# Beacon attention and soft-MoE slots: loading q and k as four rows per partition, a shorter write stride in the evacuation, earlier weight loads, output tiles in the weight slots

## The chip, the cores and the metric

The kernel runs on one core of one Trainium2 chip. The metric is the device time of one execution in microseconds, as the median of several runs. A profile is one of these executions, and its span is about 2 us shorter than the time. Each run is marked fast or slow (slow: more than 1.5% above the fastest run of the same kernel). Medians are taken over all runs.

## The reference

Causal attention with 16 beacon tokens in front, for 64 heads of 576 tokens and 64 features; then a soft mixture of experts over all 4608 tokens.

```python
# q, k, v: (8, 8, 576, 64)   beacon_k, beacon_v: (8, 8, 16, 64)   float32
scores = scale * (q @ concat([beacon_k, k]).T)        # causal over k, beacons always seen
a = softmax(scores)
x = (a @ concat([beacon_v, v])) -> (4608, 512)
logits = x @ phi                                      # phi: (512, 32), 8 experts x 4 slots
slot_input = softmax(logits, axis=0).T @ x            # 32 x 512
slot_out[e] = relu(slot_input[e] @ w1[e]) @ w2[e]     # w1: (8,512,1024), w2: (8,1024,512)
out = softmax(logits, axis=1) @ slot_out
```

TensorE needs q and k with features on the partitions, so each pair of heads is transposed. The 32 weight pieces are 1 MiB of float32 each in HBM, cast to float16 on the way. The output is 9.4 MB.

## The kernel before

A pair of heads is loaded with the 64 partitions of a head holding nine successive rows each (2304 contiguous bytes). TensorE transposes the nine 64x64 pieces per head into PSUM (the memory for TensorE's results; the kernel keeps its other tiles in SBUF), as `tp[feature, j, s]`, where token `9*s + j` is wanted. The copy to SBUF, called the evacuation below, puts the tokens in order.

```python
def load_pair(n):
    b, g = divmod(n, H // 2)
    for (d, src, nm) in ((qf, q, "qf"), (kf, k, "kf")):
        t = qkp.tile([P, J, D], FP, name=nm, tag=nm)          # J = 9, 5 buffers
        nc.sync.dma_start(out=t[:, :, :],
            in_=src[b, 2*g:2*g+2].rearrange("h s d -> (h s) d").rearrange("(p j) d -> p j d", j=J))
        d[n] = t
# ...
def transp(n):
    for (f, dst) in ((qf, qT[n % 3]), (kf, kT[n % 3])):
        t = f.pop(n)
        tp = ps_tr.tile([P, J, 64], BF, name="tr", tag="tr")
        for j in range(J):
            for po in (0, 64):
                nc.tensor.transpose(tp[po:po+64, j, :], t[po:po+64, j, :].bitcast(BF)[:, 1::2], ...)
        nc.vector.tensor_copy(                                 # writes every 9th element: 18 bytes
            out=dst[:, Nb:Nb + S].rearrange("p (s j) -> p j s", j=J), in_=tp[:, :, :])
    nc.gpsimd.tensor_copy(out=kT[n % 3][:, 0:Nb], in_=bkT[:, n, :])
# ...
for n in range(NP + 1):                    # 32 pairs; the attention of pair n-1 runs beside the scores of n
    b, g = divmod(n, H // 2)
    score(n, 0); score(n, 1)
    transp(n + 1)
    attend(n - 1, 0)                       # ends in a reciprocal and a product (xb) on VectorE
    score(n, 2)
    attend(n - 1, 1)
    # ... routing pieces of the finished batch ...
    score(n, 3)
    load_pair(n + 5)
    load_v(b + 1, g)
    for c in ((), (0, 1), (2,), (3, 4))[g]:
        cast_v(b + 1, c)                   # even c on GpSimd, odd c on VectorE
    if n % 2 == 1 and n >= 5:              # 14 weight loads, issued from GpSimd
        load_w(wl); wl += 1
# ... experts: 24 weight pieces fit in six pairs of slots, the last 8 wait for freed slots ...
for cg in range(NG):
    osb = exq.tile([P, G, Dm], FP, name="osb", tag="ex", bufs=2)
    # ... two tiles by ScalarE, two by VectorE, then a 1 MB store ...
```

The softmax here doesn't subtract the row's maximum and nothing guards it: scores larger than these inputs give would overflow.

## Time and profile before

| | before |
|---|---|
| time, median of 3 runs | 426.59 us (424.94 to 427.09) |
| span of the profiled run | 424.7 us |
| loop of 32 pairs / closing routing / experts / output | 316 / 15.8 / 41.2 / 33.7 us |
| VectorE busy | 249.9 us, of it 179 us in the 64 evacuations |

The stages, by windows cut at the events that separate them. Columns: window, length, then busy time of each engine with its number of instructions, the granted clock of TensorE, the mean share of the 16 DMA engines, and GB/s.

```profile
core 0: us, PE busy (x) PEld busy (x) DVE busy (x) ACT busy (x) POOL busy (x), PEclk, DMA share, GB/s
18.00:334.00 316.00, 173.99 (x2944) 134.95 (x2946) 222.85 (x245) 110.70 (x151) 69.38 (x131) 0.63 0.43 100
334.00:349.80 15.80, 12.12 (x192) 9.71 (x187) 6.03 (x23) 4.51 (x10) 9.38 (x13) 0.61 0.82 135
349.80:391.00 41.20, 28.39 (x323) 13.95 (x321) 0.57 (x2) 1.58 (x8) 5.82 (x8) 0.71 1.09 192
391.00:424.70 33.70, 16.74 (x37) 4.74 (x36) 13.64 (x19) 11.88 (x18) 0.00 (x0) 0.50 0.68 280
```

In the loop VectorE is the busiest engine (222.85 of 316 us), and DMA has room (share 0.43). In the expert stage the DMA share is 1.09, and waits for weights stand in the chain. Next, the chain that ended last, in one pair of the loop (start, duration, what):

```profile
...
190.21 0.64 PE tr L188 x12
...
190.88 2.70 DVE qT_128 L190
193.58 2.52 DVE kT_131 L190
...
196.16 0.50 DVE xb_141 L237
...
196.71 1.04 PE av L229 x15
...
```

Transposes, then two evacuations of 5.2 us together, then the product of the attention's first half, and only then the second half on TensorE. The records of k last 2.89 us in the mean, although the chain gives k 2.52 us, because they begin before the record of q has ended. The groups view gives the evacuations (line, engine, operation, names, shapes, count; busy us, mean ns of one; idle time before them and its cause), and the waits view gives who waits for whom (total us, times, longest):

```profile
L190 DVE COPY qT_128<-tr 128x576 bf16<-128x576 bf16 x11 | 29.8, 2707 | 14.5 <-PE tr L188 14.5
L190 DVE COPY kT_132<-tr 128x576 bf16<-128x576 bf16 x11 | 31.8, 2890 | 0.0
```

```profile
PE av L229 <- DVE xb_141 L237: 68.2, 16, 4.7
PE av L229 <- DVE xb_142 L237: 61.3, 16, 4.7
...
ACT osb L413 <- DMA out_dram<-osb: 10.6, 6, 2.1
```

TensorE loses 129 us waiting for the product, 4 us a pair. In the output stage ScalarE waits 10.6 us for stores that hold the two output buffers.

### The profile page before, as it was taken

How to read it: one execution, taken by the hardware profiler on the slowest of the kernel's cores; microseconds unless marked ns; L12 is line 12 of the kernel's file. 1: busy time of each engine (PE TensorE's matmuls, PEld its weight loads, DVE VectorE, ACT ScalarE, POOL GpSimd, SP SyncE). 2: the span in 40 equal slices, each digit the busy share in tenths (PEclk: the TensorE clock that was granted, in tenths of full speed). 3: DMA queues.
4: the chain of work that ended last, by engine and by line, in shares of the span. 5: the costliest groups of instructions: out<-in, count | busy, mean ns of one | idle time of the engine just before them, and what ended most of it. 6: DMA issues, size and time to landing. Idle time of an engine off the chain costs nothing.

```text
span 424.7 us, 8015 instructions
## 1 busy us (share of the span) xinstructions
PE 232.9 (55%) x3512; PEld 164.7 (39%) x3512; DVE 249.9 (59%) x304; ACT 129.9 (31%) x187; POOL 87.4 (21%) x161
## 2 busy tenths in 40 slices
PE   0246444555555565566556555455545779745662
PEld 0124333434443453445344444344434564412110
DVE  4477777766676766667677757775777340000442
ACT  1034333343333333342333332434333400000532
POOL 2113212121212121212123212212121342200000
PEclk9999656665666556655665565566556657955555
DMA  9953354445626452726273527450320199996687
GB/s 212 263 135 93 115 132 100 103 109 127 126 79 135 101 131 73 154 84 130 73 157 101 134 56 165 118 94 0 51 35 18 16 197 209 209 209 106 253 340 296
DMA packets 63715, 55.63 MB, mean 131 GB/s; under 512 B 41921, under 2 KB 50113, under 8 KB 62657
## 3 DMA queue, kind: packets, MB, share of 16 engines
q1 hardware_dynamic: 50880, 38.35, 31.0%
q0 software_dynamic: 12800, 16.78, 23.6%
q8 instruction: 27, 0.44, 0.4%
q14 instruction: 8, 0.06, 0.0%
HBM read 62.46 MB, written 9.44 MB: 169 GB/s over the span
## 4 chain that ended last, share of the span: by engine, by line
DVE 46%; PE 29%; DMA 15%; ACT 2%; issue 2%; SPq 2%; POOL 1%; DVEq 0%; ACTq 0%; POOLq 0%
DMA w2h<-in_moe_w_dram 11%; PE av L229 7%; DVE qT_128 L190 7%; DVE qT_129 L190 7%; DVE kT_132 L190 7%; DVE kT_131 L190 7%; DVE kT_133 L190 6%; DVE qT_130 L190 6%; PE sc_155 L202 5%; PE tr L188 4%; PE tr L256 4%; PE tr L271 3%; PE sc_154 L202 3%; DMA out_dram<-osb 3%; DVE xb_141 L237 2%
## 5 line engine op out<-in xcount | busy, mean ns | idle before, releaser
L229 PEld LDWEIGHTS <-ex 128*128 128x128 f16 (+2 forms) x960 | 55.1, 134 | 139.6 <-issue 138.0
L208 ACT ACTIVATE ex<-sc_155 128x992 f16<-128x992 f32 x64 | 48.3, 755 | 140.1 <-PE sc_155 L202 140.1
L210 POOL TENSOR_SCALAR_AFFINE_SELECT ex<-ex 128x1024 f16<-128x1024 f16 x32 | 34.9, 1089 | 248.2 <-ACT ex L208 248.2
L208 ACT ACTIVATE ex<-sc_154 128x1024 f16<-128x1024 f32 x64 | 63.0, 984 | 66.3 <-PE sc_154 L202 65.2
L229 PE MATMUL av<-vh_137,ex 128*128 128x65 f16 (+2 forms) x480 | 30.5, 234 | 68.2 <-DVE xb_141 L237 68.2
L229 PE MATMUL av<-vh_138,ex 128*128 128x65 f16 (+2 forms) x480 | 29.7, 231 | 61.3 <-DVE xb_142 L237 61.3
L190 DVE COPY qT_129<-tr 128x576 bf16<-128x576 bf16 x11 | 29.8, 2705 | 15.6 <-PE tr L188 15.6
L190 DVE COPY qT_128<-tr 128x576 bf16<-128x576 bf16 x11 | 29.8, 2707 | 14.5 <-PE tr L188 14.5
L190 DVE COPY qT_130<-tr 128x576 bf16<-128x576 bf16 x10 | 27.1, 2707 | 14.8 <-PE tr L188 14.8
L190 DVE COPY kT_132<-tr 128x576 bf16<-128x576 bf16 x11 | 31.8, 2890 | 0.0
L190 DVE COPY kT_131<-tr 128x576 bf16<-128x576 bf16 x11 | 31.8, 2889 | 0.0
L190 DVE COPY kT_133<-tr 128x576 bf16<-128x576 bf16 x10 | 28.9, 2891 | 0.0
L400 DVE TENSOR_SCALAR soh<-av,rd 32x512 f16<-32x512 f32 x1 | 0.7, 739 | 40.5 <-PE av L396 40.5
L396 PE MATMUL av<-w2h,hTz 128*32 128x512 f16 x64 | 20.6, 472 | 6.1 <-DMA w2h<-in_moe_w_dram 4.4
L188 PE MATMUL tr<-idb,qf 64*64 64x64 bf16 x576 | 20.8, 232 | 0.0
L188 PEld LDWEIGHTS <-qf 64*64 64x64 bf16 x576 | 16.6, 142 | 10.2 <-issue 10.2
L188 PE MATMUL tr<-idb,kf 64*64 64x64 bf16 x576 | 19.4, 225 | 0.4 <-DMA kf<-in_k_dram 0.4
L188 PEld LDWEIGHTS <-kf 64*64 64x64 bf16 x576 | 16.9, 142 | 0.5 <-DMA kf<-in_k_dram 0.5
L271 PE MATMUL tr<-xT,phih 128*32 128x288 f16 x64 | 16.8, 443 | 0.4 <-DVE xT L261 0.4
L414 DVE TENSOR_SCALAR osb<-sc_154,rc 128x512 f32<-128x512 f32 x9 | 6.8, 751 | 15.0 <-ACT osb L413 15.0
L119 POOL DMA_DIRECT2D w2h<-in_moe_w_dram x16 | 12.1, 761 | 12.1 <-DMA w2h<-in_moe_w_dram 12.1
L261 DVE COPY xT<-tr 128x1024 f16<-128x1024 f16 x16 | 11.1, 691 | 5.8 <-PE tr L256 5.8
(207 smaller groups left out, 352.2 us busy)
## 6 DMA issues: line engine op xcount, KB each, us to landing
qf<-in_q_dram SPq DMA_DIRECT2D x32, 288.0 KB, 2.9
kf<-in_k_dram SPq DMA_DIRECT2D x32, 288.0 KB, 3.7
w1h<-in_moe_w_dram POOLq DMA_DIRECT2D x16, 512.0 KB, 9.7
w2h<-in_moe_w_dram POOLq DMA_DIRECT2D x16, 512.0 KB, 12.7
out_dram<-osb SPq DMA_DIRECT2D x8, 1024.0 KB, 3.9
vf<-in_v_dram SPq DMA_DIRECT2D x24, 256.0 KB, 4.2
vf<-in_v_dram SPq DMA_DIRECT2D x8, 224.0 KB, 3.9
vf<-in_v_dram SPq DMA_DIRECT2D x8, 160.0 KB, 4.5
```

The source lines that it names most:

```text
L119: nc.gpsimd.dma_start(out=d[e][:, o:o + 2048].rearrange("p (c f) -> p c f", c=c), in_=src)
L188: nc.tensor.transpose(tp[po:po + 64, j, :], hi, idb[po:po + 64, po:po + 64])
L190: nc.vector.tensor_copy(out=dst[:, Nb:Nb + S].rearrange("p (s j) -> p j s", j=J), in_=tp[:, :, :])
L202: nc.tensor.matmul(sc[0:kn, a, col:col + un], kT[n % 3][64 * a:64 * a + 64, P * c:P * c + kn], qT[n % 3][64 * a:64 * a + 64, u0:u0 + un], ...
L208: nc.scalar.activation(ex[n][:, :, o:o + w], sc[:, :, 0:w], AF.Exp, scale=scale)
L210: nc.gpsimd.affine_select(out=ex[n][:, :, 0:512].rearrange("p a (c t) -> p a c t", c=4), in_=ex[n][:, :, 0:512].rearrange("p a (c t) -> p ...
L229: nc.tensor.matmul(av[0:m, a, i * DD:(i + 1) * DD], ex[n][0:kn, a, o:o + m], vh[b % 2][0:kn, c, h, :], start=(c == 0), stop=(c == i))
L237: nc.vector.tensor_tensor(out=xb[b % 2][:, :, h, :], in0=avv[:, :, 0:D], in1=r5[:, :].unsqueeze(2).broadcast_to([P, NCH, D]), op=AL.mult)
L256: nc.tensor.transpose(tp[:, ii, t, 0:m], xb[b % 2][0:m, i, 2 * t:2 * t + 2, :].rearrange("p h d -> p (h d)"), idh[0:m, 0:m])
L261: nc.vector.tensor_copy(out=xT[b][:, :, P * cs[0]:P * cs[0] + 2 * P].rearrange("p t (i u) -> p i t u", i=2), in_=tp[:, :, :, :])
L271: nc.tensor.matmul(lp[0:NSL, 0:w], phih[:, t, :], xT[b][:, t, Nb + hf * w:Nb + (hf + 1) * w], start=(t == 0), stop=(t == NDC - 1))
L396: nc.tensor.matmul(sop[0:NSL, 0, :], hTz[:, e, t, :], w2h[e][:, t * Dm:(t + 1) * Dm], start=(e == 0 and t == 0), stop=(e == E - 1 and t == ...
```

## The change

Its intent has three parts, called A, B and C below.

- A: load tokens 0 to 511 of each head as four rows per partition, in two blocks, and the last 64 tokens as one row per partition. The evacuation then writes with an 8-byte instead of an 18-byte stride, and the rest contiguously.
- B: issue 20 instead of 14 weight loads in the loop, so that fewer remain for the expert stage.
- C: take the output tiles from the six slots of the first weight matrix, instead of two buffers.

```diff
-            nc.sync.dma_start(
-                out=t[:, :, :],
-                in_=src[b, 2 * g:2 * g + 2].rearrange("h s d -> (h s) d").rearrange(
-                    "(p j) d -> p j d", j=J))
+            for a in range(2):
+                hs = src[b, 2 * g + a]
+                nc.sync.dma_start(
+                    out=t[64 * a:64 * a + 64, 0:8, :].rearrange("p (c j) d -> p c j d", j=4),
+                    in_=hs[0:512].rearrange("(c p j) d -> p c j d", p=64, j=4))
+            nc.sync.dma_start(out=t[:, 8, :],
+                              in_=src[b, 2 * g:2 * g + 2, 512:S, :])
...
             nc.vector.tensor_copy(
-                out=dst[:, Nb:Nb + S].rearrange("p (s j) -> p j s", j=J), in_=tp[:, :, :])
+                out=dst[:, Nb:Nb + 512].rearrange("p (c s j) -> p c j s", c=2, j=4),
+                in_=tp[:, 0:8, :].rearrange("p (c j) s -> p c j s", j=4))
+            nc.vector.tensor_copy(out=dst[:, Nb + 512:Nb + S], in_=tp[:, 8, :])
...
-            if n % 2 == 1 and n >= 5:
+            if n % 3 != 2 and n >= 3 and wl < 24:
                 load_w(wl)
...
-        osb = exq.tile([P, G, Dm], FP, name="osb", tag="ex", bufs=2)
+        osb = wh.tile([P, G, Dm], FP, name="osb", tag="w1h")
```

## The prediction

> **What bounds the kernel now.** Three stages follow each other (chain of waits in order of time): a start of 18 us, the 32-pair attention loop to 334 us, then the slot experts to 391 us and the output to 424.7 us.
>
> *Loop, about 9.8 us a pair.* Its chain is VectorE: the two strided evacuations of the transposed q and k (2.70 us and 2.53 us more; groups view: 2.71 and 2.89 us each, 64 of them, 179 of VectorE's 250 us), then reciprocal and product, 0.8 us; only then does TensorE run the second half of the attention. The waits view shows TensorE idle for this product 32 times, 129 us in all, 3.9 us in the pair at 187 us. In such pairs the granted clock is 0.50.
> *Experts, 349 to 391 us.* DMA share about 1.1: 14 weight loads were issued in the loop, 18 remain, and each takes 2.5 us. With weights present an expert takes 3.07 us of TensorE (timeline).
> *Output, 33.7 us.* Two output buffers: ScalarE waits 10.6 us for stores. Without that wait a group takes 2.7 us.
>
> **What the change does.**
> 1. Each evacuation becomes 512 elements at an 8-byte write stride and 64 contiguous ones. Now it costs 4.4 ns an element at 18 bytes. The Trainium skill, "SBUF — State Buffer", Door 1, says that SBUF has 16-byte lines and wants at least two hits a line; 18 bytes gives one, 8 bytes two. This trace has no 8-byte case, but a 512-element single-rate VectorE op from PSUM takes 0.74-0.75 us in it. Estimate: 0.70 us and 0.15 us for the rest, so q and k take about 1.6 us instead of 5.2.
> 2. Critical share: the product is ready 3.6 us sooner; TensorE's own work covers some 0.6 us of that, so about 3.3 us a pair come off at today's clock. Then TensorE is the limit (transposes, attention, scores: 5.5 us at clock 0.5), ScalarE has 3.5 us. Since gaps shrink to about 1 us, the clock should rise (the skill, "TensorE: Matmul & The Clock Gate", Part 1: idle windows throttle it; here the 15-matmul group takes 1.05 us at the low and 0.66 us at the high clock). I expect 5.9-6.5 us a pair, loop about 198 us instead of 316.
> 3. Costs: 16384 descriptors of 1 KB and 8192 of 256 B replace 8192 of 2304 B, and half-partition transfers. DMA for q/k may go from about 55 to 70-95 us (estimate). With v (about 55 us) and 20 weight loads (50 us) a loop of 198 us is 80-95% full: close to becoming the limit. The start has 8 more issues of 0.4 us ahead of the phi load on which VectorE waits: +3 us.
> 4. 20 loads in the loop; 12 remain, 8 of them gated by slots of experts 0 and 1. Expert stage: about 25 us instead of 41.
> 5. Six output buffers: no store wait; 29-30 us.
>
> Sum: start 21.5, loop to 220, closing routing 14, experts 25, output 30, so 291 in the profile's span, 2 more as timed, 3 for DMA contention.
>
> **Predicted: 296 us, range 270 to 330.** Faster by over 2%: 0.98; within 2%: 0.01; slower: 0.01.
>
> **What would show it.** Evacuations at 0.6-0.8 us; VectorE busy 125-140 us; TensorE's waits for the product under 1.5 us a pair; clock in the loop above 0.64; no wait of ScalarE for stores; TensorE waits for weights only at experts 6 and 7.
>
> **What would make it wrong.** The 8-byte stride still pays per line (1.2 us each: pairs of 7.4 us, 330 us in all). Or q/k loads of 64 partitions run at half rate, transposes wait for DMA and the loop is DMA-bound (310-330). Or the clock goes to full in the whole loop and pairs fall to 5 us (270).

## The result, and the profile after

| | before | after |
|---|---|---|
| time, median of 4 runs each | 426.18 us | 314.97 us (313.11 to 317.47) |
| ratio | | 0.7396 (95%: 0.7338 to 0.7453) |
| span | 424.7 us | 312.3 us |
| VectorE busy | 249.9 us | 164.7 us |
| start to the first q copy | 17.9 us | 22.0 us |

A ratio here and below is the mean time of one kernel's fast runs over that of the other's in the same rounds, so it is not quite the ratio of the quoted medians. The stages after, in the same columns as before:

```profile
core 0: us, PE busy (x) PEld busy (x) DVE busy (x) ACT busy (x) POOL busy (x), PEclk, DMA share, GB/s
22.00:240.00 218.00, 161.04 (x2940) 125.41 (x2940) 137.16 (x309) 109.64 (x150) 74.72 (x137) 0.70 0.77 163
240.00:254.80 14.80, 10.97 (x193) 8.84 (x192) 6.02 (x23) 4.56 (x10) 4.97 (x7) 0.73 0.87 149
254.80:283.00 28.20, 24.38 (x324) 13.06 (x322) 0.61 (x3) 1.58 (x8) 5.78 (x8) 0.90 1.03 175
283.00:312.30 29.30, 16.13 (x36) 4.36 (x35) 14.11 (x19) 12.31 (x18) 0.00 (x0) 0.52 0.79 322
```

The loop gave 98 us, the expert stage 13 us, the output 4.4 us, the closing routing 1 us; the start took 4 us more. The chain in one pair of the changed loop:

```profile
...
142.17 0.64 PE tr L191 x18
...
142.83 1.30 DVE qT_148 L193
144.14 0.03 DVE qT_148 L196
144.16 1.14 DVE kT_151 L193
...
145.40 0.50 DVE xb_161 L242
...
145.94 1.04 PE av L234 x15
...
```

The order of the chain is the same; the two evacuations now take 2.5 us in place of 5.2. The groups and the waits:

```profile
L193 DVE COPY qT_149<-tr 128x512 bf16<-128x512 bf16 x11 | 14.4, 1306 | 14.5 <-PE tr L191 14.4
...
L193 DVE COPY kT_151<-tr 128x512 bf16<-128x512 bf16 x11 | 14.1, 1285 | 0.0
```

```profile
POOL vh_158 L248 <- DMA vf<-in_v_dram: 33.8, 10, 6.4
POOL vh_157 L248 <- DMA vf<-in_v_dram: 31.5, 8, 6.7
...
PE av L234 <- DVE xb_162 L242: 24.8, 15, 3.4
PE av L234 <- DVE xb_161 L242: 23.7, 16, 2.0
```

Two things stand out against the prediction. A copy takes 1.30 us, not 0.70. And a wait appears that the profile before does not have among its longest: GpSimd, which casts v, waits 65 us for v to arrive. At one place this wait stands in the chain (start, duration, what):

```profile
53.44 9.89 DMA vf<-in_v_dram
```

No wait of ScalarE for stores is left.

### The profile page after: what moved, and what is told of

Same layout as the page of the kernel before. It is cut to its first block, busy times and chain, and to the rows that moved or that the text cites. A ratio compares the mean times of both kernels' runs of the same rounds, so it can differ in the third digit from the quotient of the medians.

```text
span 312.3 us, 8209 instructions
## 1 busy us (share of the span) xinstructions
PE 214.2 (69%) x3512; PEld 153.0 (49%) x3512; DVE 164.7 (53%) x368; ACT 129.4 (41%) x187; POOL 88.3 (28%) x161
## 3 DMA queue, kind: packets, MB, share of 16 engines
q1 hardware_dynamic: 68416, 38.35, 45.6%
## 4 chain that ended last, share of the span: by engine, by line
PE 40%; DVE 36%; DMA 10%; SPq 4%; ACT 4%; issue 3%; POOL 1%
PE av L234 9%; PE sc_175 L207 6%; DMA w2h<-in_moe_w_dram 6%; PE tr L191 5%; PE tr L276 5%; DVE qT_149 L193 5%; PE tr L261 4%; DVE qT_148 L193 4%; DVE kT_152 L193 4%; DVE qT_150 L193 4%; DVE kT_151 L193 4%; DVE kT_153 L193 4%; PE sc_174 L207 3%; DVE xb_162 L242 3%; DMA vf<-in_v_dram 3%; DVE xb_161 L242 3%
## 5 line engine op out<-in xcount | busy, mean ns | idle before, releaser
L234 PEld LDWEIGHTS <-ex 128*128 128x128 f16 (+2 forms) x960 | 50.1, 126 | 58.3 <-issue 56.6
L234 PE MATMUL av<-vh_157,ex 128*128 128x65 f16 (+2 forms) x480 | 29.0, 228 | 23.7 <-DVE xb_161 L242 23.7
L234 PE MATMUL av<-vh_158,ex 128*128 128x65 f16 (+2 forms) x480 | 25.9, 216 | 24.9 <-DVE xb_162 L242 24.8
L193 DVE COPY qT_149<-tr 128x512 bf16<-128x512 bf16 x11 | 14.4, 1306 | 14.5 <-PE tr L191 14.4
L193 DVE COPY qT_148<-tr 128x512 bf16<-128x512 bf16 x11 | 14.4, 1309 | 10.9 <-PE tr L191 10.8
L191 PE MATMUL tr<-idb,qf 64*64 64x64 bf16 x576 | 20.1, 227 | 0.0
L193 DVE COPY qT_150<-tr 128x512 bf16<-128x512 bf16 x10 | 13.1, 1309 | 12.9 <-PE tr L191 12.9
L401 PE MATMUL av<-w2h,hTz 128*32 128x512 f16 x64 | 17.1, 412 | 3.7 <-ACT hTz L399 2.3
L248 POOL CAST vh_158<-vf 128x512 f16<-128x512 f32 (+1 forms) x12 | 7.4, 614 | 33.9 <-DMA vf<-in_v_dram 33.8
L248 POOL CAST vh_157<-vf 128x512 f16<-128x512 f32 (+1 forms) x12 | 7.3, 614 | 31.5 <-DMA vf<-in_v_dram 31.5
L276 PE MATMUL tr<-xT,phih 128*32 128x288 f16 x64 | 15.1, 403 | 0.4 <-DVE xT L266 0.4
L175 PE MATMUL tr<-idb,bkd 128*128 128x128 bf16 x8 | 1.0, 311 | 20.0 <-DVE bkd L172 20.0
L122 POOL DMA_DIRECT2D w1h<-in_moe_w_dram x16 | 11.5, 722 | 9.6 <-PE tr L396 9.6
L193 DVE COPY kT_151<-tr 128x512 bf16<-128x512 bf16 x11 | 14.1, 1285 | 0.0
L193 DVE COPY kT_152<-tr 128x512 bf16<-128x512 bf16 x11 | 14.1, 1284 | 0.0
```

The source lines that it names most:

```text
L122: nc.gpsimd.dma_start(out=d[e][:, o:o + 2048].rearrange("p (c f) -> p c f", c=c), in_=src)
L191: nc.tensor.transpose(tp[po:po + 64, j, :], hi, idb[po:po + 64, po:po + 64])
L193: nc.vector.tensor_copy(out=dst[:, Nb:Nb + 512].rearrange("p (c s j) -> p c j s", c=2, j=4), in_=tp[:, 0:8, :].rearrange("p (c j) s -> p c ...
L234: nc.tensor.matmul(av[0:m, a, i * DD:(i + 1) * DD], ex[n][0:kn, a, o:o + m], vh[b % 2][0:kn, c, h, :], start=(c == 0), stop=(c == i))
L248: (nc.vector if c % 2 else nc.gpsimd).tensor_copy(out=vh[b % 2][0:kn, c, :, 0:D], in_=vf[(b, c)][0:kn])
L276: nc.tensor.matmul(lp[0:NSL, 0:w], phih[:, t, :], xT[b][:, t, Nb + hf * w:Nb + (hf + 1) * w], start=(t == 0), stop=(t == NDC - 1))
```

## The experiments

Twelve kernels ran; all ratios are against the kernel before in the same rounds.

| run | edit | median us | ratio (95%) |
|---|---|---|---|
| a_only | A alone | 326.87 | 0.7625 (0.7590 to 0.7660) |
| b_only | B alone | 411.65 | 0.9677 (0.9644 to 0.9710) |
| c_only | C alone | 422.62 | 0.9934 (0.9906 to 0.9962) |
| stride4 | changed kernel, 2 rows per partition | 307.39 | 0.7215 (0.7183 to 0.7248) |
| stride16 | changed kernel, 8 rows per partition | 390.99 | 0.9162 (0.9111 to 0.9212) |
| read_strided | changed kernel, stride on the PSUM side | 304.24 | 0.7135 (0.7100 to 0.7170) |
| old_load | changed kernel, loads as before (wrong token order) | 301.20 | 0.7071 (0.7042 to 0.7099) |
| rest_split | changed kernel, 8 load issues a pair | 338.96 | 0.7970 (0.7920 to 0.8020) |
| rest_act | changed kernel, rest issued from ScalarE | 321.49 | 0.7496 (0.7451 to 0.7541) |
| v_first | changed kernel, v issued before q and k | 309.45 | 0.7249 (0.7196 to 0.7302) |
| one_line | kernel before, copy walked the other way | 272.94 | none given, see text |
| best | one_line with B and C | 256.03 | none given, see text |

### The three parts, each alone

a_only carries the first two hunks of the diff, b_only the third, c_only the fourth.

> The kernel before with the new loads and evacuations alone (14 weight loads in the loop, two output buffers). If the parts add up: the loop gains what it gained in the changed kernel, about 97 us less 4 us at the start, while the expert stage stays at about 41 us and the output at 33.7 us: 330 to 336 us. If the extra weight loads in the loop cost as much in the loop as they save later (DMA contention): under 326 us.

> The kernel before with 20 instead of 14 weight loads in the loop, nothing else. Its loop is far from full on DMA (share 0.42), so the loads should be free there: the expert stage falls from 41 us to about 28 us, the loop stays within 2 us: 411 to 416 us. If weight loads in the loop delay v or q/k: 418 us or more.

> The kernel before with the output tiles in the six weight slots, nothing else: no wait of ScalarE for stores, the output stage 29.3 instead of 33.7 us, the kernel 421 to 423 us. If the stores themselves are the limit, no change: 425 to 427 us.

B alone shortened the expert stage from 41 to 27 us (the last expert matmul ends 376.2 instead of 391.0 us into the run) and left the loop as it was: as expected. C alone removed the wait for stores and is worth 0.7%, as expected. The fast runs of A alone take 324.4 us on average, 101 us less than the kernel before. That is under 326 us, the branch of its expectation in which the extra weight loads cost in the loop what they save later. The runs bear this out in part: the parts act in different stages, so their savings should add, to 27.6% of the time before, and all three together save 26.0%. About 7 us are lost, with some 3 us of doubt from the intervals. They lie in the loop. In the profiled fast runs the last attention matmul ends 239.5 us into a_only and 246.4 us into the changed kernel, and GpSimd waits 24.6 us for v in a_only and 65 us in the changed kernel. The six more weight loads in a shorter loop are not free.

### What the evacuation pays for

Theory L: a strided write pays for each 16-byte line of SBUF that it opens. Rival A: only the alignment of the 18-byte stride was bad. Rival B: the cost belongs to the source or to any strided walk. The edit of stride4 and stride16 replaces four rows per partition by two and by eight:

```diff
-  "(c p j) d -> p c j d", p=64, j=4        # and j=4 in the three other patterns, c=2
+  "(c p j) d -> p c j d", p=64, j=2        # stride4: c=4, 4-byte write stride, 512-byte descriptors
+  "(c p j) d -> p c j d", p=64, j=8        # stride16: c=1, 16-byte write stride, 2 KB descriptors
```

and read_strided keeps the loads and turns the walk round, so that SBUF is written contiguously:

```diff
-   out=dst[:, Nb:Nb + 512].rearrange("p (c s j) -> p c j s", c=2, j=4),
-   in_=tp[:, 0:8, :].rearrange("p (c j) s -> p c j s", j=4))
+   out=dst[:, Nb:Nb + 512].rearrange("p (c s j) -> p c s j", c=2, j=4),
+   in_=tp[:, 0:8, :].rearrange("p (c j) s -> p c s j", j=4))
```

> The changed kernel with 2 rows per partition instead of 4: 512-byte descriptors, 4-byte write stride (4 elements in a 16-byte line). Theory L (a strided write pays about 4.4 ns for each 16-byte line that it opens; 8 bytes: 2 elements a line, hence 2.2 ns an element): the 512-element copy falls from 1.30 to 0.70-0.75 us, the loop loses 0.6 to 1 us a pair, and the kernel takes 287 to 300 us unless the smaller descriptors give it back. Rival A (only the alignment matters: 18 bytes is no multiple of 4; every aligned non-unit stride costs 2.2 ns an element): the copy stays at 1.30 us and the kernel at 312 to 320 us.

> The changed kernel with 8 rows per partition: 2 KB descriptors, 16-byte write stride (one element in a line, aligned). Theory L: 512 lines at 4.4 ns, so the copy takes 2.3 to 2.5 us, nearly as slow an element as before the change, and the kernel 365 to 390 us. Rival A (alignment): the copy stays at 1.30 us and the kernel at 308 to 318 us.

> The changed kernel, but the copy walks the transposed tile in token order: it reads PSUM with a 128-byte step and writes SBUF contiguously. Same elements, same load. Theory L (the cost sits on the SBUF write side): no strided write is left, so the copy takes 0.6 to 0.8 us, and the kernel 287 to 300 us. Rival B (the cost belongs to the 16-bit PSUM source or to the strided walk wherever it is): 1.30 us or more, the kernel 315 us or slower.

The groups view of the three, stride4 first:

```profile
L193 DVE COPY qT<-tr 128x512 bf16<-128x512 bf16 x32 | 23.6, 737 | 51.7 <-PE tr L191 51.5
L193 DVE COPY kT<-tr 128x512 bf16<-128x512 bf16 x32 | 23.0, 719 | 0.0
```

Then stride16:

```profile
L193 DVE COPY kT<-tr 128x512 bf16<-128x512 bf16 x32 | 80.7, 2523 | 0.0
L193 DVE COPY qT<-tr 128x512 bf16<-128x512 bf16 x32 | 78.4, 2449 | 42.6 <-PE tr L191 42.6
```

Then read_strided:

```profile
L193 DVE COPY qT<-tr 128x512 bf16<-128x512 bf16 x32 | 22.1, 690 | 47.5 <-PE tr L191 47.3
L193 DVE COPY kT<-tr 128x512 bf16<-128x512 bf16 x32 | 21.8, 681 | 0.1
```

| q copy | elements | 16-byte lines opened | mean ns |
|---|---|---|---|
| contiguous write, PSUM read with a 128-byte step | 512 | 64 | 690 |
| 4-byte stride | 512 | 128 | 737 |
| 8-byte stride | 512 | 256 | 1306 |
| 16-byte stride | 512 | 512 | 2449 |
| 18-byte stride (before) | 576 | 576 | 2707 |

From 128 to 256 lines the copy takes 569 ns more, which is 4.4 ns a line; from 256 to 512 lines 1143 ns, 4.5 ns a line; from 512 to 576 lines 258 ns, 4.0 ns a line. (The k copies of the same views give 4.4 to 5.7 ns a line. Where copies are long their records start before the q copy has ended, so the q copies are used here.) An aligned 16-byte stride costs as much per element (4.8 ns) as the misaligned 18-byte one (4.7 ns), so rival A falls. The copy with the stride on the PSUM side takes 690 ns, so rival B falls too. Theory L stands, and read_strided adds what the change did not use: with the walk turned round, the reordering costs no strided write at all.

The kernel times of stride4 and read_strided missed their expectation (287 to 300 us): they are 307.4 and 304.2 us; stride16 is 1 us above its range. In stride4 and read_strided the waits of GpSimd for v rose to 102.5 and 90.1 us, and waits for v make up 21.0% and 19.9% of the chain, against 3% in the changed kernel. The faster copy ran into the next limit: the arrival of v.

### Why v comes late

Theory D put it down to the new form of the loads as a whole. The run old_load keeps everything but takes the old loads back. Its layout is wrong: the evacuation expects the new one, so tokens of q and k come out in another order. The check passed it all the same. Passing the check does not prove the token order in this case; for the other runs the order follows from the edits.

> Wrong result on purpose: the changed kernel with the old loads of q and k (one 2304-byte descriptor a partition, one transfer over 128 partitions), evacuated as in the changed kernel. Theory D (the smaller descriptors and half-partition transfers make the transfers so long that the v loads come late, and that stretches the loop): the waits of GpSimd for v fall from 65 us to under 35 us, the first q copy starts 3 to 4 us earlier, and the kernel takes 300 to 308 us. Rival: the loop is bound by VectorE and TensorE alone, only the start comes earlier: 310 to 312 us.

It took 301.2 us, about 14 us less than the changed kernel. The first q copy starts at 18.0 instead of 22.0 us, and waits of GpSimd for v are gone from its list. So the new loads cost about 14 us, of which 4 us lie in the start. The bytes are the same. By the packet times, the hardware queue, which carries q, k and v and also the stores of the output, took 44.2% of 299.4 us in old_load and 45.6% of 312.3 us in the changed kernel, 132 against 142 us of all 16 engines: 10 us more, and in the loop the mean share is 0.77, not full. What differs far more is the queue that issues the loads. Its timeline (start, duration, what; x2 is two issues in one row), in old_load:

```profile
...
152.85 0.35 SPq L87 DMA_DIRECT2D qf<-in_q_dram  x1
153.33 0.35 SPq L87 DMA_DIRECT2D kf<-in_k_dram  x1
153.77 0.38 SPq L102 DMA_DIRECT2D vf<-in_v_dram  x1
```

and in the changed kernel:

```profile
...
154.31 3.49 SPq L89 DMA_DIRECT2D qf<-in_q_dram  x2
157.85 0.81 SPq L92 DMA_DIRECT2D qf<-in_q_dram  x1
158.76 2.48 SPq L89 DMA_DIRECT2D kf<-in_k_dram  x2
161.28 0.53 SPq L92 DMA_DIRECT2D kf<-in_k_dram  x1
161.91 0.41 SPq L105 DMA_DIRECT2D vf<-in_v_dram  x1
...
```

Summed over the loop from such timelines, issuing took about 175 of 218 us in the changed kernel and about 45 us in old_load. A half-pair issue takes 0.61 to 0.62 us in the median where one for a whole pair took 0.33 us (q) or 0.38 us (k), and the longest took 3.55 us. With the median of each kind for every issue of the loop the sum would be about 120 us (an estimate from the traced durations). The other 55 us lie in issues that took longer than usual.

Three more runs asked what in this delays v. Theory S: the issuing sequencer is the limit. Theory E: the single rest transfer has the two heads as the slowest dimension of its source, and by the Trainium skill, "DMA: Bandwidth & Descriptors", section "Why a DMA increments its semaphore by 16 and not by 1", the number of engines must divide that dimension, so it would run on 2 of 16. The records do not name the engine, but the trace agrees: in the changed kernel each of the 64 single rest transfers left 3 updates of its semaphore, every other load 16, and in rest_split all loads left 16. So the rest probably ran on few engines; the question is whether that delays v.

rest_split makes the rest two transfers of one head each:

```diff
-            nc.sync.dma_start(out=t[:, 8, :], in_=src[b, 2 * g:2 * g + 2, 512:S, :])
+            for a in range(2):
+                nc.sync.dma_start(out=t[64 * a:64 * a + 64, 8, :], in_=src[b, 2 * g + a, 512:S, :])
```

> The changed kernel, with the rest transfer (row 8 of both heads, 128 descriptors of 256 bytes) issued as two transfers of one head each. Same descriptors, two more issues a pair. Theory E (the source of the single rest transfer has the two heads as its slowest dimension, so it runs on 2 of the 16 DMA engines; 64 such transfers at 19.6 ns a descriptor put some 80 us on those two, and the v loads behind them come late): with 64 rows as the slowest dimension it spreads, the waits of GpSimd for v fall from 65 us to under 35 us, and the kernel takes 303 to 310 us. Theory S (the sequencer that issues the loads is busy nearly all the time, and the v loads are issued late): two more issues a pair make it worse, 317 us or more, the waits for v 65 us or more.

rest_act issues it from ScalarE's queue:

```diff
-            nc.sync.dma_start(out=t[:, 8, :],
+            nc.scalar.dma_start(out=t[:, 8, :],
```

> The changed kernel, with the rest transfer issued from ScalarE's queue instead. Theory S: the loading sequencer has two issues of six fewer a pair, the waits for v fall below 35 us, and the kernel takes 304 to 311 us. Theory E: the same two DMA engines carry the rest, the waits for v stay above 50 us, and the kernel at 312 to 320 us.

v_first moves `load_v(b + 1, g)` ahead of `load_pair(n + 5)` in the loop, with nothing else changed.

> The changed kernel with one reordering: in each iteration the loads of v are issued before the six of q and k instead of after them. Same transfers, same queue. Theory S (the loading sequencer is busy issuing for 175 of the loop's 218 us, so v, cast one pair later, is issued late, while q and k are five pairs ahead and can bear a delay): the waits of GpSimd for v fall from 65 us to under 25 us, and the kernel takes 303 to 311 us. Rival (the transfers as a whole, or the sequencer as a whole, can't keep up): the wait moves to TensorE waiting for q and k, 312 us or more.

The waits for v, of rest_split:

```profile
POOL vh L249 <- DMA vf<-in_v_dram: 123.2, 21, 10.0
DVE vh L249 <- DMA vf<-in_v_dram: 18.9, 7, 7.8
```

of rest_act, where ScalarE's own waits for loads are shown too:

```profile
POOL vh L248 <- DMA vf<-in_v_dram: 25.6, 9, 5.7
...
ACT ex L213 <- DMA kf<-in_k_dram: 19.4, 8, 4.3
...
ACT ex L213 <- DMA qf<-in_q_dram: 7.5, 4, 3.8
```

of v_first:

```profile
POOL vh L248 <- DMA vf<-in_v_dram: 64.5, 18, 9.9
```

The loading queue of rest_act waits too, for transfers to land that were issued earlier:

```profile
SPq L89 <- DMA qf<-in_q_dram: 34.2, 14, 4.8
SPq L105 <- DMA kf<-in_k_dram: 20.9, 7, 5.5
```

rest_split made it 24 us worse, against theory E. With 8 issues a pair the waits for v are 142 us, GpSimd and VectorE together. With 6 issues (changed kernel) they are 68 us, with 4 on that queue (rest_act) 28 us, with 2 (old_load) they are not in the list. And v is not carried more slowly: from issue to landing a v load takes 4.9 us in the median of rest_split (2.7 to 9.1) and 5.2 us in old_load (3.5 to 9.4). It is issued late, as theory S says. The number of issues is not all, though. With the same 6 issues the waits of GpSimd for v are not in the list of stride16, whose pair takes 9.4 us, are 24.6 us in a_only, and 90.1 and 102.5 us in read_strided and stride4. So the pace of the loop and the weight loads count as well. Nor does old_load change the issues alone: its descriptors are larger and its transfers span all partitions.

The time of rest_act did not follow theory S: it was expected at 304 to 311 us, and its fast runs take 318.9 us on average. That lies in the range given for theory E, but the waits for v do not (E: above 50 us). Its issues now stand between the activations of ScalarE, which waits 27 us in the loop for loads of q and k, and the loading queue waits about 70 us for earlier transfers of q, k and v to land. The wait was moved, not removed. v_first fell inside the time that theory S gave (309.5 us), but not by its mechanism: the waits for v stayed at 64.5 us. So it is not the order inside one iteration that makes v late; the queue as a whole is behind. What makes the issues long that took more than their usual 0.6 us, back-pressure of the half-partition transfers or something else, these runs do not separate; that stays open.

### The statement that does more than the change

read_strided shows that the copy needs no help from the load's layout. Then the old loads can stay, and one statement of the kernel before is enough:

```diff
             nc.vector.tensor_copy(
-                out=dst[:, Nb:Nb + S].rearrange("p (s j) -> p j s", j=J), in_=tp[:, :, :])
+                out=dst[:, Nb:Nb + S].rearrange("p (s j) -> p s j", j=J),
+                in_=tp[:, :, :].rearrange("p j s -> p s j"))
```

one_line is the kernel before with this alone; best has it with B and C.

> The kernel before with one statement changed: the evacuation walks the transposed tile in token order, so that it reads PSUM with a step and writes SBUF contiguously; old loads, 14 weight loads in the loop, two output buffers. If the reading side is free as the read-strided run says: 576 elements in 0.70 to 0.80 us, a pair of 5.5 to 6.2 us, and the kernel 296 to 310 us, below the changed kernel though its expert stage and output stay as they were. If the read-strided walk was cheap only for rows of four: 1.3 us or more a copy and the kernel above 315 us.

> That same statement with the old loads, and with the other two parts of the change (20 weight loads in the loop, output tiles in the weight slots). Relative to the old-load run (301.2 us) two copies of 1.53 us become two of 0.75 us; TensorE hides part of it: 280 to 292 us, and few waits for v. If the loop is bound by DMA by then, 293 us or more with waits for v above 35 us.

The outputs are right. Their token order follows from the edit (position 9*s + j is read from tp[:, j, s]), and both beat their expectation: one_line 272.94 us (268.07 to 274.37), best 256.03 us (250.13 to 258.24). Their runs spread by more than 1.5%, so no ratio was given. Even the slowest runs are far below the changed kernel's 313 to 317 us. The 17 us between the two medians agree with B and C alone (13.6 and 2.6 us), but this spread allows no finer reading. The groups and the loop's window of one_line, whose profiled run is fast:

```profile
L190 DVE COPY qT<-tr 128x576 bf16<-128x576 bf16 x32 | 24.2, 757 | 26.3 <-PE tr L188 26.0
L190 DVE COPY kT<-tr 128x576 bf16<-128x576 bf16 x32 | 24.0, 749 | 0.9 <-PE tr L188 0.8
```

```profile
16.40:177.00 160.60, 125.47 (x2911) 99.43 (x2912) 102.84 (x242) 107.09 (x147) 69.44 (x131) 0.93 0.85 199
```

576 elements take 0.75 us. A pair takes 5.0 us in place of 9.9. It was expected at 5.5 to 6.2 us. TensorE's longest wait for the product is 1.0 us instead of 4.7, the granted clock in the loop is 0.93, and with the old loads the DMA share goes to 0.85 with 1.2 us of waiting for v in all.

## Why the prediction was right or wrong

The kernel became faster as predicted, and 314.97 us lies in the range of 270 to 330 us. The point, 296 us, was 19 us too low. Part of this closeness is luck, because two errors pulled against each other. The copies and loads cost more than predicted; but the pair that the prediction gave for fast copies, 5.9 to 6.5 us with TensorE as the limit, was too long: with copies of 0.75 us and no late v, one_line takes 5.0 us a pair. Term by term:

- *The bound.* Right. The loop's chain ran through the two evacuations; shortening them alone (read_strided's statement put into the kernel before) took 153 us.
- *"Estimate: 0.70 us and 0.15 us for the rest."* This is the step that was wrong, by its size: 1.28 to 1.31 us and 0.22 us were measured. The term "q and k take about 1.6 us" was 2.5 us in the chain. The prediction took from the Trainium skill, "SBUF — State Buffer", Door 1, that two hits in a 16-byte line suffice; stride4, stride16 and read_strided show that each line costs 4.4 to 4.5 ns between 128 and 512 lines, and the copy came near the 0.69 us of a contiguous write only with four two-byte elements in a line (0.74 us). The prediction named this case as its first risk, with 1.2 us a copy. It is worth about 11 us of the changed kernel's time (read_strided: 304.2 us), as long as v is late.
- *"3 for DMA contention" and the start's "+3 us".* The start was right (4 us). The loop's share was mis-sized: about 10 of the 14 us that the new loads cost (old_load). The named risk was right that half-partition loads could bind, but the wait showed on v, which the busy loading queue issued late, and not on the transposes.
- *The clock.* The direction was right: 0.63 before, 0.70 after, 0.78 in old_load, 0.93 in one_line. The Trainium skill ties this to idle windows ("TensorE: Matmul & The Clock Gate", Part 1). These loops agree in part: TensorE's waits for the product are 129, 48.5, 48.6 and 25.7 us in the same order, so the changed kernel and old_load differ in clock at the same sum of waits. The pairs were 6.8 us (218 us over 32), not 5.9 to 6.5.
- *Experts.* 28 us, not 25. GpSimd waits 9.6 us for expert 0 to free the first slot and 2.7 us more for its second matrix before it can issue the last loads.
- *Output.* Right: 29.3 us, no wait for stores.
- *Signs.* The wait for the product was to be under 1.5 us a pair and was 1.6 (48.5 us in 31 waits); VectorE busy was to be 125 to 140 us and was 165, which is the copies again.

What stays open is why some issues of the loading queue take far longer than their median.

## What to carry to other kernels

When a VectorE copy of two-byte elements out of PSUM reorders them, try to put the stride on the reading side and write SBUF contiguously, before any load is reshaped to shorten a write stride. When loads are cut into more transfers, count the issues of their queue per iteration as a cost of its own: here 6 in place of 2 kept the queue busy for 80% of the loop, and the loads that came late were those of v. When a chain that TensorE waits for is shortened, look at the granted clock again before the next estimate: here it rose from 0.63 to 0.93, and pairs became shorter than expected.

## What the Trainium skill lacked or had wrong

- "SBUF — State Buffer", Door 1, says that two hits in a 16-byte line give full bandwidth, so that eight bf16 may be stepped over for free. For VectorE writes of bf16 this does not hold: 8 bytes took 1.31 us, 16 bytes 2.45 us, against 0.69 us contiguous and 0.74 us at 4 bytes, for 512 elements. The runs give a cost of 4.0 to 4.5 ns a line.
- The same section warns of non-contiguous PSUM access, for matmuls. The warning should not be carried over to VectorE's reads: 576 two-byte elements read with a 128-byte step took 0.75 us.
- "DMA: Bandwidth & Descriptors", section "Issuing engines are not separate DMA queues", calls the sequencer's time to initiate a DMA usually small relative to the DMA itself. Added up it was not small here: issuing took about 175 us of a 218 us loop, at 0.61 to 0.62 us for a half-partition transfer of 128 descriptors against 0.33 to 0.38 us for one of 128 descriptors over 128 partitions. No page gives the cost of an issue by its shape.
